# One read of the first batch's x, turned on TensorE; a weight conversion spread over three engines; a newly chosen instruction order

## The chip, the core and the metric

The kernel runs on one core of a Trainium2 chip. The core has five queues that run side by side, each strictly in its own order: TensorE (PE: matrix products and transposes, writing to PSUM), VectorE (DVE), ScalarE (ACT: functions of a table, and copies), GpSimd (POOL) and SyncE (SP), which here issues all DMA transfers. The metric is the device time of one execution in microseconds, median of several runs.

## What is computed

The reference is an attention through 32 inducing points over four batches of 12,480 tokens of 128 numbers, and behind it a two-layer network with a rational activation over all 49,920 tokens:

```python
def mab(q, kv):
    s = scale * (q @ kv.transpose(0, 2, 1))
    s = s - s.max(-1, keepdims=True)
    a = np.exp(s)
    a /= a.sum(-1, keepdims=True) + 1e-09
    return a @ kv
h = mab(I, x)                       # 32 points look at all tokens of a batch
x = mab(x, h)                       # every token looks at the 32 points
h = x @ w_in                        # 128 -> 2048
P = a[0] + a[1] * h + a[2] * h2 + a[3] * h3          # h2 = h*h, h3 = h2*h
Q = 1.0 + np.abs(b[0]) * np.abs(h) + np.abs(b[1]) * h2
out = (P / (Q + 1e-6)) @ w_out      # 2048 -> 128
```

`w_in` and `w_out` come as 64-bit floats and are turned into 32-bit ones on the chip, by work on their bits.

## The kernel before

A batch is cut into 26 tiles of 480 tokens (`BT`), four chunks of 120 each; seven groups of up to four tiles make the 32 points of a batch.

**The start** (`before`, lines 1235 to 1251, then `main` up to line 1292) is written out by hand and kept in program order (`pin`). For batch 0 x is read twice: by columns (`wide_columns`, `x_c`, 128 channels on the partitions) for the scores, and by rows (`wide_rows`, `x_t`, tokens on the partitions) for the weighted sum. For each group, `score` multiplies the points with the columns into the PSUM tile `pc`, takes the maximum on DVE (`mx`, `nm`), the exponential on ACT (`e`) and turns it with four PE transposes (`pt`, copied to `eT`); `weigh` multiplies `eT` with the rows (`ph`) and DVE adds to `acc`. `level`, the division and a last product give `HT0`, the points. Between these steps `step` deals out the conversion of the weights (`convert_weights`): four parts of `w_in` of 480 columns and one of 128, five parts of `w_out` of 384 and one of 128, seven DVE instructions each, the tiles named `cv` and `cw`. `warm` lets PE multiply the identity (`spare`) where it would wait. When the points are there, a flag decides on the branch; all that follows is the branch `main(True)`. It converts the last two parts of `w_out`, makes the first tokens' attention (`tokens`, `pd`, `a`, `pa`, `at`), the first pieces of the stacked first layer (`pg`, `gs`, `st`), scales `w_out` by a number (line 1287) and hands over to the flow.

**The block** (`Flow`) is all the rest: 832 units, each one tile of 480 tokens and two of the 16 row blocks of the hidden layer. PE makes `h` (two products, `first`); |h| goes to a buffer of `rooms` by ACT (`abs`) or, for the masked half of the units, by DVE (`mask`) or ACT (`taken`); DVE multiplies (`D`) into a slot `l`. A masked unit needs a constant added first: either POOL does it (`pre`, a tensor_scalar `l<-rooms,all`), or PE adds it to `h` with two more products with a constant matrix (`shift`, `h<-at,bump`). ACT takes a logarithm over one to four rooms at once (`ln`; a room holds two units, 1920 columns), and behind a change of function table a sigmoid: over a room (`sig2`), over one unit (`sig`), or into PSUM (`sigp`, tile `i`). Units whose sigmoid is in PSUM are ended by DVE (`Ev`), the others by two POOL instructions (`add`, `Eg`). PE multiplies with `w_out` (`second`, tile `po`, four records per unit). Attention for later tokens and batches is mixed in.

Which engine takes what, and in which order, is decided while the program is built, by `Flow.run`: it keeps a clock for each engine, moves it on by `COST`, and of what is ready picks by the weights `RANK`, `GEN`, `WAIT` and `LOAD`, of which a row of `SETS` is put in force for each 16 units (`PLAN`). The tables change only the order and the choice among `shift` and `pre`, `mask` and `taken`, `Ev` and `Eg`, `ln` over one room or several.

## Time and profile before

| | |
|---|---|
| median of 3 runs | 2232.44 us (2232.06 to 2234.06) |
| the profiled execution | 2232.32 us, span of its instructions 2230.4 us |
| busy: PE, DVE, ACT, POOL | 97%, 91%, 95%, 86% of the span |
| weight loads of PE (PEld) | 55% |
| chain that ended last | PE 48%, ACT 18%, POOL 15%, DVE 9%, issue 6%, DMA 2% |
| DMA | 82.59 MB read, 25.56 MB written |

Busy is the union of the instructions' durations, whatever they wait for inside. Neighbouring instructions of DVE and ACT overlap in the records by some 0.06 to 0.1 us; where the distance from start to start matters, it is read from a list in order of time. A PE record's end is modelled; the granted clock of PE is given as a share of 2.4 GHz, so 0.5 is 1.2 GHz.

### The profile page before, as it was taken

How to read it: one execution, taken by the hardware profiler on the slowest of the kernel's cores; microseconds unless marked ns; L12 is line 12 of the kernel's file. 1: busy time of each engine (PE TensorE's matmuls, PEld its weight loads, DVE VectorE, ACT ScalarE, POOL GpSimd, SP SyncE). 2: the span in 40 equal slices, each digit the busy share in tenths (PEclk: the TensorE clock that was granted, in tenths of full speed). 3: DMA queues.
4: the chain of work that ended last, by engine and by line, in shares of the span. 5: the costliest groups of instructions: out<-in, count | busy, mean ns of one | idle time of the engine just before them, and what ended most of it. 6: DMA issues, size and time to landing. Idle time of an engine off the chain costs nothing.

```text
span 2230.4 us, 24813 instructions
## 1 busy us (share of the span) xinstructions
PE 2158.1 (97%) x8210; PEld 1236.5 (55%) x8210; DVE 2028.7 (91%) x2208; ACT 2108.8 (95%) x1646; POOL 1917.0 (86%) x1279
## 2 busy tenths in 40 slices
PE   6899999999999999999999999999999999999998
PEld 3555555555655555655555555555555555555554
DVE  8798998999889999998999998989999999999996
ACT  2699999999999999999999999999999999999996
POOL 0479999997999898988899989999789989799884
PEclk9799999999999999999999999999999999999999
DMA  8122221211121212222112222221110111011000
GB/s 331 49 83 65 80 63 60 67 45 36 45 80 46 64 55 62 75 70 64 45 36 62 77 78 62 81 64 55 54 36 27 45 45 45 22 42 36 27 27 20
DMA packets 76937, 135.20 MB, mean 61 GB/s; under 512 B 13312, under 2 KB 63616, under 8 KB 76800
## 3 DMA queue, kind: packets, MB, share of 16 engines
q1 hardware_dynamic: 76800, 133.52, 19.2%
q8 instruction: 68, 1.11, 0.2%
q14 instruction: 69, 0.57, 0.1%
HBM read 82.59 MB, written 25.56 MB: 48 GB/s over the span
## 4 chain that ended last, share of the span: by engine, by line
PE 48%; ACT 18%; POOL 15%; DVE 9%; issue 6%; DMA 2%; SPq 0%; POOLq 0%; DVEq 0%; ACTq 0%
PE po L166 30%; POOL l L166 15%; ACT rooms L166 13%; PE h L166 11%; DVE l L166 6%; ACT i L166 3%; PE pd L166 2%; DVE rooms L166 2%; DMA rooms<-x_t 2%; PE ph L166 2%; ACT L166 1%; PE pc L166 1%; PE pl L166 1%; PE pgt L166 0%; DVE oT L166 0%
## 5 line engine op out<-in xcount | busy, mean ns | idle before, releaser
L166 PE MATMUL po<-l,w_out 128*128 128x480 f32 x3328 | 1466.4, 571 | 7.1 <-DVE oT L166 4.9
L166 POOL TENSOR_TENSOR l<-l,rooms 128x960 f32<-128x960 f32 x506 | 1136.0, 2245 | 71.5 <-ACT rooms L166 37.6
L166 PEld LDWEIGHTS po<-l,w_out 128*128 128x128 f32 x3328 | 616.3, 190 | 500.8 <-issue 435.9
L166 DVE SCALAR_TENSOR_TENSOR l<-rooms,all,h 128x960 f32<-128x960 f32 x648 | 770.7, 1206 | 55.2 <-ACT rooms L166 23.9
L166 ACT ACTIVATE rooms<-rooms,all 128x1920 f32<-128x1920 f32 (+3 forms) x286 | 743.4, 2621 | 3.9 <-POOL l L166 3.2
L166 PE MATMUL h<-at,st 128*128 128x480 f32 x1664 | 631.7, 475 | 29.6 <-DVE l L166 26.0
L166 POOL TENSOR_SCALAR l<-l,all 128x960 f32<-128x960 f32 x506 | 541.8, 1071 | 2.4
L166 DVE TENSOR_SCALAR rooms<-h 128x960 int32<-128x960 int32 x413 | 474.4, 1151 | 57.7 <-PE h L166 55.3
L166 ACT ACTIVATE rooms<-h,all 128x960 f32<-128x960 f32 x416 | 434.7, 1051 | 30.6 <-PE h L166 28.6
L166 ACT ACTIVATE rooms<-rooms 128x960 f32<-128x960 f32 (+1 forms) x331 | 461.0, 1417 | 0.2
L166 PEld LDWEIGHTS h<-at,st 128*128 128x128 f32 x1664 | 296.0, 190 | 288.9 <-issue 158.5
L166 DVE SCALAR_TENSOR_TENSOR l<-l,all,i 128x960 f32<-128x960 f32 x326 | 386.5, 1206 | 21.8 <-ACT i L166 20.7
L166 ACT ACTIVATE i<-rooms 128x960 f32<-128x960 f32 x326 | 310.3, 966 | 12.8 <-DVE l L166 11.2
L166 POOL TENSOR_SCALAR l<-rooms,all 128x960 f32<-128x960 f32 x184 | 196.6, 1069 | 136.9 <-DVE rooms L166 120.8
L166 DVE SCALAR_TENSOR_TENSOR l<-h,all,l 128x960 f32<-128x960 f32 x184 | 221.6, 1208 | 13.2 <-POOL l L166 11.4
L166 ACT ACT_TABLE_LOAD x140 | 179.6, 1283 | 3.2 <-PEq L1339 0.7
L166 PE MATMUL h<-at,bump 128*128 128x480 f32 x464 | 171.8, 452 | 3.8 <-DVE rooms L166 3.8
L166 PEld LDWEIGHTS h<-at,bump 128*128 128x128 f32 x464 | 84.0, 189 | 61.7 <-issue 26.2
L166 PEld LDWEIGHTS pd<-HT,xT 128*120 128x120 f32 x832 | 104.3, 187 | 18.2 <-issue 9.1
L166 PE MATMUL pd<-HT,xT 128*120 128x32 f32 x832 | 97.9, 262 | 1.9 <-ACT gs L166 1.4
L166 DVE COPY oT<-po 128x480 f32<-128x480 f32 x104 | 67.7, 651 | 24.8 <-PE po L166 24.2
L166 PE MATMUL po<-at,st 128*128 128x480 f32 x104 | 79.1, 760 | 0.0
(114 smaller groups left out, 700.2 us busy)
## 6 DMA issues: line engine op xcount, KB each, us to landing
xT<-x_c SPq DMA_DIRECT2D x182, 240.0 KB, 3.4
out<-oT SPq DMA_DIRECT2D x104, 240.0 KB, 2.2
at<-hl SPq DMA_DIRECT2D x412, 60.0 KB, 2.0
...
rooms<-x_c SPq DMA_DIRECT2D x5, 960.0 KB, 13.3
...
```

The costliest lines, as they stand in the source:

```text
L166: ins = call(*args, **kw)
```

## The change

Batch 0 is read by rows alone (`first_rows`, nine transfers into the rooms 9 to 1, the first in three pieces). `turned` makes the columns on the chip: for each tile four PE transposes into PSUM (`px`, two tiles to a PSUM buffer), and an ACT copy of 960 columns to `xc`. It runs two groups ahead of the scores. The parts of `w_out` land in rooms 0, 9 and 8. A conversion has now five DVE instructions, one on ACT (`cw<-raw`, the low word) and two on POOL (product and sum), and the last DVE instruction of a part comes one part later. The five parts of `w_in` are dealt out in the start, five steps a group; all six parts of `w_out` are converted behind the branch, the rest of them in one go (`step(60)`), and the scaling of `w_out` moves from DVE to POOL. `COST` of most instructions is raised (`first` 0.44 to 0.48, `shift` 0.44 to 0.47, `second` 1.61 to 1.63), all rows of `SETS` are new, and `PLAN` repeats another of them.

```diff
--- before.py
+++ after.py
@@ convert_weights
-    c = pool.tile([P, width], I32, tag=tags[1], name=f"cw{name}", bufs=1)
-    V = nc.vector
+    r = pool.tile([P, 2, width], I32, tag=tags[1], name=f"cw{name}", bufs=1)
+    c, l = r[:, 0], r[:, 1].bitcast(F32)
+    V, G = nc.vector, nc.gpsimd
     af, bf = a.bitcast(F32), b.bitcast(F32)
     yield V.tensor_scalar(out=a, in0=hi, scalar1=0x07FFFFFF, scalar2=3, op0=ALU.bitwise_and, op1=ALU.logical_shift_left)
+    nc.scalar.activation(l, lo.bitcast(U32), AF.Identity, bias=0.0, scale=2.0 ** -52)
     yield V.scalar_tensor_tensor(out=a, in0=hi, scalar=-0x40000000, in1=a, op0=ALU.bitwise_and, op1=ALU.bitwise_or)
     yield V.tensor_scalar(out=b, in0=a, scalar1=-0x00800000, scalar2=None, op0=ALU.bitwise_and)
-    yield V.scalar_tensor_tensor(out=bf, in0=lo.bitcast(U32), scalar=2.0 ** -52, in1=bf, op0=ALU.mult, op1=ALU.mult)
+    G.tensor_tensor(out=bf, in0=bf, in1=l, op=ALU.mult)
+    G.tensor_tensor(out=bf, in0=bf, in1=af, op=ALU.add)
     yield V.tensor_scalar(out=c, in0=hi, scalar1=0x7FF00000, scalar2=None, op0=ALU.bitwise_and)
-    yield V.tensor_tensor(out=bf, in0=bf, in1=af, op=ALU.add)
+    yield None
     yield V.scalar_tensor_tensor(out=dst, in0=c, scalar=float(0x38100000), in1=bf, op0=ALU.is_ge, op1=ALU.mult)
@@ class Flow
-    COST = {"first": 0.44, "second": 1.61, "linear": 0.22, "fetch": 0.57, "D": 1.125, "mask": 1.067, "Ev": 1.125, "abs": 0.944, "taken": 0.85, "ln": 1.79, "sig": 1.694, "half": 0.894, "load": 1.295, "both": 3.39, "pre": 1.04, "add": 1.12, "Eg": 2.215, "shift": 0.44}
+    COST = {"first": 0.48, "second": 1.63, "linear": 0.22, "fetch": 0.58, "D": 1.14, "mask": 1.085, "Ev": 1.135, "abs": 0.953, "taken": 0.85, "ln": 1.79, "sig": 1.694, "half": 0.894, "load": 1.295, "both": 3.39, "pre": 1.05, "add": 1.155, "Eg": 2.225, "shift": 0.47}
...
-        (77.9, 124, -279.1, 100.3, -37.2, -206.1, -83.4, 15.5, 61, 42.1, -224.4, 138.8, 408.6, 142.1, 24.5, 5.2, 59.4, 108.4, -17.2, -196.8, 18.8, 155, 103.5, -281.3, 0.07, 0.06, 0.06, 0.15, 0.25, -2.08, 210.6, 102.3),
+        (69.7, 124, -262.9, 108.4, -97.4, -198.7, -83.4, 13.3, 32.6, 47.2, -213.9, 108.5, 409, 149.2, 14.2, 4.9, 76.4, 108.4, -13.5, -190.6, 17.9, 162.6, 45.1, -281.3, 0.07, 0.06, 0.06, 0.09, -0.41, -1.54, 193.5, 106.1),
...
-        self.stretch, self.near = -1, -1
+        self.stretch, self.near = -1, 0
@@ class Kernel
-    STEPS = 8, 11, 11, 11, 11, 8, 3
+    STEPS = 5, 5, 5, 5, 5, 5, 0
-        nc.sync.dma_start(out=self.ind, in_=self.ind_c)
...
-            if n == len(parts) - 2:
-                yield None
-            raw = self.mp.tile([P, width], mybir.dt.int64, tag=self.place("l"), name=f"raw{n}", bufs=1)
+            if n < 5:
+                raw = self.mp.tile([P, width], mybir.dt.int64, tag=f"l{n}", name=f"raw{n}", bufs=1)
+            else:
+                t = self.rooms[:, (0, 0, 9, 9, 8, 8)[n - 5], n % 2].rearrange("p a n -> p (a n)")
+                raw = t[:, 0:2 * width].bitcast(mybir.dt.int64)
...
+    def first_rows(self):
+        for k in range(-(-self.NB // 3)):
+            n, m = 3 * k, min(3, self.NB - 3 * k)
+            t = self.rooms[:, Flow.ROOMS - 1 - k].rearrange("p a b n -> p (a b n)")[:, 0:m * HB * C].rearrange("p (m h c) -> p m h c", h=HB, c=C)
+            for lo, hi in ([(j, j + 1) for j in range(m)] if k == 0 else [(0, m)]):
+                self.nc.sync.dma_start(out=t[:, lo:hi].rearrange("p m h c -> p (m h) c"), in_=self.x_t[0, :, HB * (n + lo):HB * (n + hi), :])
+                if k == 0:
+                    yield
+            self.rows += [t[0:TP, j] for j in range(m)]
+            yield
+    def turned(self, g):
+        nc, xs, cols = self.nc, self.rows[4 * g:4 * g + 4], []
+        for h in range(0, len(xs), 2):
+            m = min(2, len(xs) - h)
+            px = self.ps_h.tile([P, 2, 512], F32, tag=f"hp{h // 2}", name=f"px{g}_{h}", bufs=1)
+            for j in range(m):
+                for c in range(HB):
+                    nc.tensor.transpose(out=px[:, j, TP * c:TP * c + TP], in_=xs[h + j][:, c, :], identity=self.ident[0:TP, 0:TP])
+            t = self.mp.tile([P, 2, BT], F32, tag=f"l{15 + (2 * g + h // 2) % 6}", name=f"xc{g}_{h}", bufs=1)
+            nc.scalar.activation(t[:, 0:m], px[:, 0:m, 0:BT], AF.Identity, bias=0.0, scale=1.0)
+            cols += [t[:, j] for j in range(m)]
+        return cols
+    def first_scores(self, g, cols, state):
+        nc, ap, nb = self.nc, self.ap, self.count(g)
+        X, scale, rows = mybir.AxisListType.X, 1.0 / math.sqrt(C), slice(0, M * nb)
+        pc = self.ps_m.tile([P, 512], F32, tag="misc", name=f"pc0_{g}")
+        for j, t in enumerate(cols):
+            nc.tensor.matmul(pc[M * j:M * j + M, 0:BT], self.ind, t, start=True, stop=True)
+        mx = ap.tile([P, 1], F32, tag="mx", name=f"mx0_{g}")
+        nc.vector.tensor_reduce(out=mx[rows], in_=pc[rows, 0:BT], axis=X, op=ALU.max)
+        old, nm = state["nm"], ap.tile([P, 1], F32, tag="nm", name=f"nm0_{g}", bufs=2)
+        state["nm"] = nm
+        if g == 0:
+            nc.vector.tensor_scalar(out=nm, in0=mx, scalar1=-scale, scalar2=None, op0=ALU.mult)
+        else:
+            if nb < 4:
+                nc.vector.tensor_copy(out=nm, in_=old)
+            nc.vector.tensor_scalar(out=nm[rows], in0=mx[rows], scalar1=-scale, scalar2=old[rows], op0=ALU.mult, op1=ALU.min)
+        e = ap.tile([P, BT], F32, tag="e", name=f"e0_{g}")
+        sums = ap.tile([P, 1], F32, tag="sums", name=f"sums0_{g}", bufs=3)
+        nc.scalar.activation(e[rows], pc[rows, 0:BT], AF.Exp, bias=nm[rows], scale=scale, accum_out=sums[rows])
+        cor = None
+        if g:
+            cor = ap.tile([P, 1], F32, tag="cor", name=f"cor0_{g}", bufs=2)
+            nc.scalar.activation(cor[rows], old[rows], AF.Exp, bias=nm[rows], scale=-1.0)
+        return e, sums, cor
+    def first_turn(self, g, e):
+        nc, rows = self.nc, slice(0, M * self.count(g))
+        pt = self.ps_h.tile([P, 2, 512], F32, tag="hp2", name=f"pt0_{g}", bufs=1)[:, 0].rearrange("p (c n) -> p c n", c=HB)
+        for c in range(HB):
+            nc.tensor.transpose(out=pt[0:TP, c, rows], in_=e[rows, TP * c:TP * c + TP], identity=self.ident[rows, rows])
+        eT = self.ap.tile([P, 512], F32, tag="gs", name=f"eT0_{g}", bufs=2)[0:TP].rearrange("p (c n) -> p c n", c=HB)
+        nc.scalar.activation(eT[:, :, rows], pt[0:TP, :, rows], AF.Identity, bias=0.0, scale=1.0)
+        return eT
+    def first_weigh(self, g, eT, sums, cor, acc):
+        nc, V, nb = self.nc, self.nc.vector, self.count(g)
+        rows, xs = slice(0, M * nb), self.rows[4 * g:4 * g + 4]
+        ph = self.ps_o.tile([P, 512], F32, tag="po", name=f"ph0_{g}")
+        for c in range(HB):
+            for j in range(nb):
+                nc.tensor.matmul(ph[M * j:M * j + M, 0:C], eT[:, c, M * j:M * j + M], xs[j][:, c, :], start=(c == 0), stop=(c == HB - 1))
+        if g == 0:
+            V.tensor_copy(out=acc[:, 0:C], in_=ph[:, 0:C])
+            V.tensor_copy(out=acc[:, C:], in_=sums)
+        else:
+            V.scalar_tensor_tensor(out=acc[rows, 0:C], in0=acc[rows, 0:C], scalar=cor[rows], in1=ph[rows, 0:C], op0=ALU.mult, op1=ALU.add)
+            V.scalar_tensor_tensor(out=acc[rows, C:], in0=acc[rows, C:], scalar=cor[rows], in1=sums[rows], op0=ALU.mult, op1=ALU.add)
+    def first_points(self):
+        self.rows, loads = [], self.first_rows()
+        for _ in range(3):
+            next(loads)
+        self.nc.sync.dma_start(out=self.ind, in_=self.ind_c)
+        self.fetch_words(1)
+        for _ in loads:
+            self.fetch_words(len(self.raw) < 5)
+        self.fetch_words(2)
+        acc = self.ap.tile([P, C + 1], F32, tag="acc", name="acc0")
+        state = {"acc": acc, "nm": None}
+        last, cols = self.NG - 1, {0: self.turned(0), 1: self.turned(1)}
+        old = None
+        self.conversion = self.converting([self.raw.pop(0) for _ in range(5)])
+        for g in range(self.NG):
+            e, sums, cor = self.first_scores(g, cols.pop(g), state)
+            self.step(self.STEPS[g])
+            if old is not None:
+                self.first_weigh(g - 1, *old, acc)
+            self.fetch_words(2 if 1 < g < 4 else 0)
+            if g + 2 <= last:
+                cols[g + 2] = self.turned(g + 2)
+            elif g == last:
+                self.open_spare("spare0")
+                self.warm(4)
+            old = self.first_turn(g, e), sums, cor
+        level = self.level(0, state["nm"])
+        self.until_bank(level, 2)
+        self.step(60)
+        self.first_weigh(last, *old, acc)
+        self.drive(self.points(0, state, level, self.cp.tile([C, 4 * M], F32, name="HT0")))
...
-    def converting(self):
-        while True:
-            if not self.raw:
-                return
-            tags = self.place("l"), self.place("l")
-            yield from convert_weights(self.nc, self.mp, *self.raw.pop(0), self.converted, tags)
-            self.converted += 1
+    def converting(self, parts):
+        last = None
+        while parts or last is not None:
+            this = None
+            if parts:
+                tags = [f"l{11 + 2 * (self.converted % 2) + i}" for i in range(2)]
+                this = convert_weights(self.nc, self.mp, *parts.pop(0), self.converted, tags)
+                self.converted += 1
+                for done in this:
+                    if done is None:
+                        break
+                    yield
+            if last is not None:
+                next(last)
+                yield
+            last = this
@@ before, main
-        self.drive(self.induce(0, self.cp.tile([C, 4 * M], F32, name="HT0")))
+        self.first_points()
-        self.fetch_words(2)
-        self.conversion = self.converting()
+        self.conversion = self.converting(list(self.raw))
-            self.step(20)
-            nc.vector.tensor_scalar(out=self.w_out, in0=self.w_out, scalar1=p.rho, scalar2=None, op0=ALU.mult)
+            self.step(60)
+            nc.gpsimd.tensor_scalar(out=self.w_out, in0=self.w_out, scalar1=p.rho, scalar2=0.0, op0=ALU.mult, op1=ALU.add)

```

Counted in the branch taken, the new order holds (records of PE and instructions of the others):

| | before | after |
|---|---|---|
| PE `h<-at,bump` (two to a `shift`) | 464 | 386 |
| POOL `pre` | 184 | 223 |
| POOL `add` and `Eg` pairs | 506 | 491 |
| DVE `Ev`, ACT `sigp` | 326 | 341 |
| DVE `mask` / ACT `taken` | 413 / 3 | 407 / 9 |
| ACT `ln` over 1, 2, 3, 4 rooms | 190, 69, 20, 7 | 254, 55, 12, 4 |
| ACT `sig2` / `sig` | 175 / 156 | 157 / 177 |
| ACT copies to `eT`, on 120x512 (the rest by DVE) | 27 | 35 |

How the start moves is shown at three places. On PE, around the third group's scores in the start, before (`pc` scores, `ph` weighted sums, `pt` turned exponentials; L166 and L169 are the line of the helper that records every instruction):

```order
L166 MATMUL pc_2_217<-rooms,ind 32x480 x4
L166 MATMUL ph_1_246<-rooms,eT_1_208 32x128 x16
L166 MATMUL pt_2_265<-ident,e_2_226 120x128 x4
L166 MATMUL pc_3_276<-rooms,ind 32x480 x4
L166 MATMUL ph_2_303<-rooms,eT_2_270 32x128 x16
```

The same place after (`px` are the transposes of x, `xc` the copies of them that the scores read):

```order
L169 MATMUL pc_2_295<-xc_0_203,ind 32x480 x2
L169 MATMUL pc_2_295<-xc_2_214,ind 32x480 x2
L169 MATMUL ph_1_319<-rooms,eT_1_293 32x128 x16
L169 MATMUL px_0_340<-ident,rooms 128x120 x8
L169 MATMUL px_2_351<-ident,rooms 128x120 x8
L169 MATMUL pt_2_362<-ident,e_2_304 120x128 x4
L169 MATMUL pc_3_369<-xc_0_275,ind 32x480 x2
L169 MATMUL pc_3_369<-xc_2_286,ind 32x480 x2
```

Sixteen transposes have come between the weighted sum of one group and the turned exponentials of the next. On DVE behind the branch, from the first token's attention to the first instruction of the block (`TENSOR_SCALAR rooms<-h` is the first `mask`), before:

```order
L166 TENSOR_TENSOR at_0_0_705<-pa_0_696,at_0_0_705 32x480 x2
L166 TENSOR_SCALAR cv_723<-raw_656 128x128
L166 SCALAR_TENSOR_TENSOR cv_723<-raw_656,cv_723 128x128
L166 TENSOR_SCALAR cv_723<-cv_723 128x128
L166 SCALAR_TENSOR_TENSOR cv_723<-raw_656,cv_723 128x128
L166 TENSOR_SCALAR cw_724<-raw_656 128x128
L166 TENSOR_TENSOR cv_723<-cv_723 128x128
L166 SCALAR_TENSOR_TENSOR w_out<-cw_724,cv_723 128x128
L166 TENSOR_SCALAR w_out<-w_out,all 128x2048
L166 TENSOR_SCALAR rooms<-h_0_2_742 128x960
```

The same place after: 23 conversion instructions stand between `at` and the first `mask`, of which these are the last eleven:

```order
L169 TENSOR_SCALAR cv_847<-rooms 128x384
L169 SCALAR_TENSOR_TENSOR cv_847<-rooms,cv_847 128x384
L169 TENSOR_SCALAR cv_847<-cv_847 128x384
L169 TENSOR_SCALAR cw_848<-rooms 128x384
L169 SCALAR_TENSOR_TENSOR w_out<-cw_838,cv_837 128x384
L169 TENSOR_SCALAR cv_857<-rooms 128x128
L169 SCALAR_TENSOR_TENSOR cv_857<-rooms,cv_857 128x128
L169 TENSOR_SCALAR cv_857<-cv_857 128x128
L169 TENSOR_SCALAR cw_858<-rooms 128x128
L169 SCALAR_TENSOR_TENSOR w_out<-cw_848,cv_847 128x384
L169 SCALAR_TENSOR_TENSOR w_out<-cw_858,cv_857 128x128
L169 TENSOR_SCALAR rooms<-h_0_2_878 128x960
```

The seven conversion instructions and the scaling between `at` and the first `mask` have become 23 conversion instructions. On POOL behind the branch, up to the first `pre` (`TENSOR_SCALAR l<-rooms,all`), before:

```order
L166 TENSOR_TENSOR bump<-level,bump 64x128
L166 TENSOR_TENSOR st_645<-gs_0_686,st_645 64x512
L166 TENSOR_TENSOR st_645<-gs_1_712,st_645 64x512
L166 TENSOR_SCALAR l_0_0_750<-rooms,all 128x960
L166 TENSOR_SCALAR l_0_2_755<-rooms,all 128x960
```

And after, the last twelve rows up to the first `pre`:

```order
L169 TENSOR_TENSOR cv_799<-cv_799,cw_800 128x384
L169 TENSOR_TENSOR cv_799<-cv_799 128x384
L169 TENSOR_TENSOR cv_827<-cv_827,cw_828 128x384
L169 TENSOR_TENSOR cv_827<-cv_827 128x384
L169 TENSOR_TENSOR cv_837<-cv_837,cw_838 128x384
L169 TENSOR_TENSOR cv_837<-cv_837 128x384
L169 TENSOR_TENSOR cv_847<-cv_847,cw_848 128x384
L169 TENSOR_TENSOR cv_847<-cv_847 128x384
L169 TENSOR_TENSOR cv_857<-cv_857,cw_858 128x128
L169 TENSOR_TENSOR cv_857<-cv_857 128x128
L169 TENSOR_SCALAR w_out<-w_out,all 128x2048
L169 TENSOR_SCALAR l_0_0_886<-rooms,all 128x960
```

Before the first `pre` POOL has now twelve conversion products and sums and the scaling of `w_out` over 2048 columns.

## Rows read from the trace of the kernel before

**Rows 1.** Chain that ended last, by engine, from the page.

```profile
PE 48%; ACT 18%; POOL 15%; DVE 9%; issue 6%; DMA 2%; SPq 0%; POOLq 0%; DVEq 0%; ACTq 0%
```

**Rows 2.** Windows: stretch, length, busy us of PE, PEld, DVE, ACT, POOL; clock, DMA, GB/s.

```profile
0.00:10.00 10.00, 3.07 (x8) 0.55 (x8) 4.28 (x63) 1.69 (x3) 0.68 (x6) 1.00 0.56 191
20.00:30.00 10.00, 8.15 (x74) 3.95 (x66) 9.61 (x21) 2.13 (x5) 0.00 (x0) 1.00 1.03 417
160.00:2200.00 2040.00, 2005.15 (x7413) 1144.63 (x7413) 1885.58 (x1891) 1998.65 (x1528) 1851.99 (x1226) 1.00 0.18 54
```

**Rows 3.** Chain that ended last, in order of time: start, length, what.

```profile
30.21 13.35 DMA rooms<-x_t
```

**Rows 4.** PE in order of time, start: start, length, instructions.

```profile
39.95 1.11 PE L166 MATMUL pt<-ident,e 128*120 128x128 f32 x4
...
44.60 0.66 PE L166 MATMUL pt<-ident,e 128*120 128x128 f32 x4
45.19 1.00 PE L166 MATMUL pc<-rooms,ind 128*32 128x480 f32 x4
46.12 1.60 PE L166 MATMUL spare<-ident 128*128 128x128 f32 x12
47.66 1.08 PE L166 MATMUL ph<-rooms,eT 120*32 120x128 f32 x32
```

**Rows 5.** DVE in order of time, from the end of the start on.

```profile
48.70 0.54 DVE L166 TENSOR_TENSOR cv<-cv 128x384 f32<-128x384 f32 x1
...
54.94 0.29 DVE L166 COPY HT<-HT 128x128 f32<-128x128 f32 x1 [0.64 <-PE HT L166]
...
56.13 0.56 DVE L166 SCALAR_TENSOR_TENSOR cv<-raw,cv 128x384 int32<-128x384 int32 x1
56.73 0.36 DVE L166 TENSOR_SCALAR cv<-cv 128x384 int32<-128x384 int32 x1
...
59.68 1.63 DVE L166 TENSOR_TENSOR cv<-cv 128x384 f32<-128x384 f32 x1
...
65.49 1.98 DVE L166 TENSOR_SCALAR w_out<-w_out,all 128x2048 f32<-128x2048 f32 x1
...
68.45 1.20 DVE L166 SCALAR_TENSOR_TENSOR l<-rooms,all,h 128x960 f32<-128x960 f32 x1
```

**Rows 6.** POOL in order of time, the same stretch.

```profile
59.52 1.37 POOL L166 TENSOR_TENSOR st<-gs,st 64x512 fp32r<-64x512 f32 x1 [5.33 <-ACT st L166]
...
65.27 1.12 POOL L166 TENSOR_SCALAR l<-rooms,all 128x960 f32<-128x960 f32 x1 [1.47 <-DVE cv L166]
```

**Rows 7.** POOL groups, 160 to 2200 us: count, busy us, mean ns, idle before.

```profile
L166 POOL TENSOR_TENSOR l<-l,rooms 128x960 f32<-128x960 f32 x494 | 1109.2, 2245 | 67.9 <-ACT rooms L166 34.9 <-POOL l L166 0.2
...
L166 POOL TENSOR_SCALAR l<-rooms,all 128x960 f32<-128x960 f32 x172 | 183.8, 1069 | 105.5 <-DVE rooms L166 92.8 <-PE po L166 6.5 <-ACT rooms L166 4.5
```

**Rows 8.** PE in order of time, in the block: one shift and what follows.

```profile
1016.47 0.60 PE L166 MATMUL h<-at,bump 128*128 128x480 f32 x2
1016.90 0.56 PE L166 MATMUL po<-l,w_out 128*128 128x480 f32 x1
```

**Rows 9.** ACT groups, 160 to 2200 us.

```profile
L166 ACT ACTIVATE rooms<-h,all 128x960 f32<-128x960 f32 x399 | 417.0, 1051 | 20.8 <-PE h L166 18.8 <-issue 0.3
L166 ACT ACTIVATE rooms<-rooms,all 128x1920 f32<-128x1920 f32 x179 | 335.7, 1893 | 3.8 <-POOL l L166 3.2 <-DVE l L166 0.4
L166 ACT ACTIVATE rooms<-rooms 128x1920 f32<-128x1920 f32 x170 | 302.8, 1795 | 0.2
L166 ACT ACTIVATE i<-rooms 128x960 f32<-128x960 f32 x309 | 294.2, 965 | 9.8 <-DVE l L166 8.5
L166 ACT ACTIVATE rooms<-rooms,all 128x3840 f32<-128x3840 f32 x68 | 237.5, 3494 | 0.0
...
L166 ACT ACTIVATE rooms<-rooms 128x960 f32<-128x960 f32 x153 | 151.8, 992 | 0.0
```

**Rows 10.** DVE group of `Ev`, 160 to 2200 us.

```profile
L166 DVE SCALAR_TENSOR_TENSOR l<-l,all,i 128x960 f32<-128x960 f32 x309 | 366.7, 1207 | 17.4 <-ACT i L166 16.2
```

More of the change, by code (lines that the diff above doesn't have):

```diff
@@ L741, in score @@
             nc.tensor.matmul(pc[M * j:M * j + M, 0:BT], self.ind, t, start=True, stop=True)
-        if not self.boot:
-            yield "unring", 0
+        yield "unring", 0
         yield "v", 0.57
@@ L757, in score @@
         e = ap.tile([P, BT], F32, tag="e", name=f"e{b}_{g}")
[L758 to L762 removed]
+        nc.scalar.activation(e[rows], pc[rows, 0:BT], AF.Exp, bias=nm[rows], scale=scale)
         yield "free", 0
@@ L868, in induce, with points @@
             yield from self.weigh(b, g, xs, state)
-        level = self.level(b, state["nm"])
-        if self.boot:
-            self.until_bank(level, 2)
-            self.step(20)
-            self.warm(1)
-            self.drive(self.weigh(b, self.NG - 1, rs[4 * self.NG - 4:], state))
+        yield from self.points(b, state, self.level(b, state["nm"]))
+    def points(self, b, state, level, own=None):
+        nc, ap, acc = self.nc, self.ap, state["acc"]
         cor = yield from level
@@ L999, in tokens @@
             for j in range(nb):
-                yield "pe", 0.75
+                yield "pe", 0.9
                 if j == 0:
```

59 lines of the change are left out of this document (5 added, 54 removed), and 98 rows, old and new, of the table SETS.

## The prediction

> **What bounds the kernel now.** I read the page first, then windows, the chain of waits, each engine's groups, and last the lists in order of time around the start. The page's chain goes to and fro: PE 48%, ACT 18%, POOL 15%, DVE 9% [rows 1], so no single engine sets the block. The windows say how little each could give back: of the 2040 us from 160 to 2200, PE is busy 2005, ACT 1999, DVE 1886, POOL 1852 [rows 2]. PE's figure is partly made by modelled ends; ACT's is real work, so ACT has 41 us of pause and is at least as tight as PE. The start is another case: from 10 us on the DMA share is full at 417 GB/s [rows 2], and the chain of waits is a transfer of x from 30.21 to 43.56 [rows 3]. The points are there with the copy of `HT` at 54.94, and the first product of the block on DVE begins at 68.45 [rows 5].
>
> Three terms follow: when the points are there, how long after them the block begins, and how long the block takes. The sum is made against the profiled execution, 2232.3 us, which is 0.1 below the median.
>
> **Term one, the points.** Reading x once takes 6.8 MB out of the queue: x by rows and `w_in` are 8.9 MB by their shapes. With 1.91 MB moved in the first 10 us and 0.417 MB/us from there [rows 2], all of x is in SBUF at 27 us instead of 43.6. But the scores of the first group stand on PE behind the transposes of the second, whose last tiles have 3.85 MB up to and with them in the queue: 14.7 us, and the first scores at about 15.9. From there PE has, for a group, the scores (0.93, from 45.19 to 46.12), the weighted sum (1.08), four transposes of exponentials (0.59, from 44.60 to 45.19) and sixteen new ones, by the same row 4 x 0.59 = 2.4: 4.9 us [rows 4]. ACT has two new copies of 960 columns, by the nearest group about 1.05 each [rows 9], which still leaves its group below PE's. Four groups at 4.9, one with half the transposes at 3.7, and one without at 3.3 (there the round from PE over DVE and ACT and back sets the time) bring the last scores to 42.5; before they began at 45.19. From there to `HT` it was 9.75 us, of which 1.5 were the warm-up products from 46.12 to 47.66 [rows 4, 5]; so `HT` would come at 50.7, 4.2 earlier. That holds at PE's full pace. The four transposes took 1.11 us at 39.95 and 0.66 at 44.60 [rows 4]: 1.7 times as long while PE still paused for x. At that pace throughout, the groups cost some 18 us more and `HT` is 14 late. PE would now pause little from 16 us on, as it did around 45; I let one group of the six run at the slow pace (3.4 us) and take **-1**, with ends at -5 and +8.
>
> **Term two, from the points to the block.** Here stands what the start has put off: all six parts of `w_out`, 30 DVE instructions instead of 14, and 12 POOL instructions instead of none. DVE alone: a part of 384 columns has three tensor_scalars at 0.36 and two of two inputs at 0.56 [rows 5]; less 0.08 of overlap each that is 1.8 us, 9.9 for the six parts with the narrow one. Before it was 2.8 and 1.4 for two parts, and 1.1 for the scaling without its wait: 5.3. So DVE's own work grows by 4.6. POOL: a product of two inputs over 960 columns takes 2.245 [rows 7], so I estimate 0.9 over 384, and 9.6 us for the twelve. The two cannot run beside each other freely. The DVE sum over 384 columns took 0.54 at 48.70, with POOL idle, and 1.63 at 59.68, while POOL's instruction of 59.52 ran for 1.37; the scaling took 1.98 at 65.49, beside POOL's of 65.27 [rows 5, 6]: DVE began when POOL was done, both times. These are a sum of two SBUF inputs and a one-input tensor_scalar; no row shows a scalar_tensor_tensor beside POOL. If all five of a part are held, DVE and POOL take turns: 9.9 and 9.6, and about 4 us of first-token work and 1 of waits, put the first `mask` at some 24 us behind `HT` and the first product at 25.5; before it was 13.5. That is +12. If only the three tensor_scalars are held, it is +9. If none is, POOL's own queue sets it, about 5 us until its first product, two splits of 1.37 and 9.6: the first product 19 us behind, +5.5. I take **+11**, the ends are +5 and +15. What hid the work before was the long transfer of x, beside which DVE converted; that cover is gone. Behind it POOL still scales `w_out` (1.069 x 2048/960 = 2.3 us [rows 7]) ahead of the first `pre`; DVE's first masks and the units without a mask need no `pre` and hide it, so I count nothing; without that cover it is 2.3.
>
> The Trainium skill, SBUF — State Buffer, section "Who interferes with whom", has a rule on this: a DVE instruction with two SBUF inputs, or in a mode that uses both ports, is locked out for the whole of a GpSimd instruction that reads SBUF, and the other way round. The two waits above agree; by the rule all five instructions of a part are held, and the term would be +12.
>
> **Term three, the block.** 39 shifts leave PE; two products and on to the next take 0.43 [rows 8], so PE loses 16.8 us. POOL gains 39 `pre` and loses 15 pairs: 39 x 1.07 - 15 x (2.245 + 1.07) = -8 [rows 7], the second figure of a pair by the form of `pre`. DVE gains 15 `Ev` at 1.2 [rows 10] and gives up six masks and eight copies, some +8. ACT grows: 39 logarithms more over the same 416 rooms, each split costing 2 x 1.893 - 3.494 = 0.29, are 11 at most and 8 with the overlap taken out; 15 sigmoids to PSUM and 21 single ones for 18 over a room are 15 x 0.965 + 21 x 0.992 - 18 x 1.795 = +3; six `taken` at 1.05 are 6; copies shifted between ACT and DVE about +1 [rows 9]. Together +18 on an engine with 41 us of pause. So PE's relief is a gain of up to 17 and ACT's load a loss of up to 18, on two engines that are alike in pause; I put the term at **0**, with both as ends.
>
> The sum: -1 + 11 + 0 = +10, **2242 us**. Its own range, with term two at its ends and term three within 4, is 2234 to 2252.
>
> **Rivals.**
> PE sets the block. For it: half the chain is PE, and its products with `w_out` come first in that chain [rows 1]. Against it: ACT would need to run with 23 us of pause where it has 41. Then 17 come back; with the points 4 early and the block beginning +6 to +8 behind them, the time is 2232 - 17 - 4 + 7 = 2218; with a part of the relief lost, 2221. This is the faster case, and it decides from 10 us of relief on.
>
> ACT sets the block. For it: 1999 of 2040 busy, and its largest pauses are 19 us for PE's `h` and 9 for DVE [rows 9], so little is left to squeeze. Then the term is +18 and the time 2260, or 2257 if the points come at -4.
>
> The Trainium skill's front page (Trainium Kernel Development and Optimization, "Performance Expectations") calls matmul busy time a bad measure and weight-load time a good one. By the weight loads, 1145 of 2040, PE is far from full, which speaks for this rival.
>
> The two cancel: the block gives back 10 and the start takes it, 2232. The change of the read then does what it says and is not seen.
>
> The start gains as it was cut to: no holding between DVE and POOL, PE at full pace, -5 and +5 in the first two terms. With term three at 0 that is 2232 too, and I count it with the case above.
>
> **How the numbers follow.** Forecast 0.41, PE sets the block 0.27, ACT sets it 0.17, cancelled 0.15. What a measurement of this kernel can tell from no change is about 0.2%, 4.5 us. The forecast's own range begins at +2, so a small part of it (0.03) is no change, and a part of the cancelled case (0.02) is faster. Faster 0.29, within 0.2% 0.16, slower 0.55. The range leaves out a tenth on each side: 2215, where PE's relief comes back whole and the points are early, to 2260, where ACT sets the block.
>
> **What would show it.** Term one: the `HT` copy on DVE, forecast at 54, and the distance of the scores `pc` from group to group, 4.9 us at full pace. Term two: the distance from there to the first product `l<-rooms,all,h`, 24 to 26 us, with conversions on DVE of 1 us and more where 0.36 and 0.56 are their own, lying against POOL's products. Term three: the time from the first `po` to the end, and ACT's pause between 160 and 2200, forecast at no more than 30 us. I am wrong if `HT` comes before 50, if the first product comes less than 19 us behind it, or if the block alone is more than 8 us shorter or longer.

## The result, and the profile after

The changed kernel takes 2259.36 us (median of 4 runs, 2257.45 to 2260.51) against 2232.57: the ratio is 1.0118, with a 95% interval from 1.0101 to 1.0136. It is slower, as forecast, but by 26.8 us where +10 was forecast. The profiled execution took 2257.45 us with a span of 2255.6, 25.2 more than before; it is the fastest of the four, so the spans below account for 25 of the 26.8 us.

Two points cut that span into the prediction's three terms: the copy of `HT` on DVE, and the first product on DVE behind it.

| | before | after | term | forecast |
|---|---|---|---|---|
| `HT` copied | 54.94 | 55.03 | +0.1 | -1 (-5 to +8) |
| from there to the first product | 13.51 | 26.16 | +12.65 | +11 (+5 to +15) |
| from there to the end of the span | 2161.95 | 2174.41 | +12.5 | 0 (-17 to +18) |

The windows of the kernel after (stretch, length, busy us of PE, PEld, DVE, ACT, POOL; clock, DMA, GB/s), which answer to [rows 2]; the row of 81.19 begins at the first product and is the block:

```profile
20.00:30.00 10.00, 8.95 (x122) 6.50 (x121) 9.32 (x19) 7.67 (x14) 5.22 (x4) 1.00 1.02 409
70.00:80.00 10.00, 0.06 (x1) 0.06 (x1) 8.85 (x16) 3.76 (x7) 6.14 (x7) 0.50 0.00 0
81.19:2255.60 2174.41, 2116.03 (x7750) 1200.37 (x7750) 1976.57 (x1986) 2102.85 (x1668) 1905.03 (x1280) 0.99 0.18 54
160.00:2200.00 2040.00, 1997.88 (x7342) 1130.31 (x7341) 1881.46 (x1887) 2006.43 (x1588) 1830.76 (x1229) 1.00 0.18 54
```

And the same stretch, from the first product on, of the kernel before:

```profile
68.45:2230.40 2161.95, 2112.33 (x7825) 1210.27 (x7825) 1972.06 (x1982) 2088.53 (x1600) 1912.08 (x1269) 0.99 0.18 54
```

In the block PE has 75 records less and is busy 3.7 us *longer*; its pauses have grown from 49.6 to 58.4. ACT is busy 14.3 longer and pauses 1.9 less: seen from ACT, the block has grown by ACT's own work. That this work is the cause is not shown by these two rows; it is tested below. From 160 to 2200, ACT pauses 33.6 us (41 before). The chain of the page, by engine, answers to [rows 1]; ACT's share was 18%:

```profile
PE 40%; ACT 30%; DVE 13%; issue 9%; POOL 8%; DMA 1%; SPq 0%; DVEq 0%; ACTq 0%; POOLq 0%
```

The groups of ACT from 160 to 2200 (count, busy us, mean ns, idle before) show where its work comes from, against [rows 9]: logarithms over one room, and sigmoids of one unit:

```profile
L169 ACT ACTIVATE rooms<-rooms,all 128x1920 f32<-128x1920 f32 x242 | 454.0, 1894 | 3.5 <-DVE l L169 3.0 <-DVE nm L169 0.3
...
L169 ACT ACTIVATE i<-rooms 128x960 f32<-128x960 f32 x319 | 302.7, 964 | 10.7 <-DVE l L169 9.6
L169 ACT ACTIVATE rooms<-rooms 128x1920 f32<-128x1920 f32 x151 | 269.3, 1796 | 0.2
L169 ACT ACTIVATE rooms<-rooms,all 128x3840 f32<-128x3840 f32 x55 | 192.2, 3497 | 0.1
L169 ACT ACTIVATE rooms<-rooms 128x960 f32<-128x960 f32 x171 | 169.7, 993 | 0.0
```

One group of the start on PE (start, length, instructions), which answers to [rows 4], and the last scores:

```profile
25.29 1.86 PE L169 MATMUL px<-ident,rooms 120*128 120x120 f32 x16
26.98 0.60 PE L169 MATMUL pt<-ident,e 128*120 128x128 f32 x4
27.52 1.01 PE L169 MATMUL pc<-xc,ind 128*32 128x480 f32 x8
28.74 1.08 PE L169 MATMUL ph<-rooms,eT 120*32 120x128 f32 x32 [0.21 <-ACT eT L169]
29.75 1.86 PE L169 MATMUL px<-ident,rooms 120*128 120x120 f32 x16
...
45.32 1.00 PE L169 MATMUL pc<-xc,ind 128*32 128x480 f32 x4
```

The scores stand 4.5 to 5.1 us apart, as forecast (4.9), at the full clock. But the first came at 17.87 instead of 15.9, and the last are 9.7 from `HT`, as before; the 1.5 that I took off for the warm-up products did not come, since PE waits there for the exponentials and not for itself. So the early read was lost in full against this profile of before. That profile is the earliest of its kind, though: in the nine runs below whose start is word for word that of before, `HT` is copied between 55.06 and 57.84, and with the one before the ten have a mean of 55.9. The changed start puts it between 54.82 and 55.07 in four runs. In the old start the granted clock lies at 0.5 for 7 to 24 us of the first 50, while PE pauses for x; in the changed one it is 1.00 up to 60.

Behind the points, on DVE: `HT`, one part of `w_out`, and the first product, against [rows 5]:

```profile
55.03 0.29 DVE L169 COPY HT<-HT 128x128 f32<-128x128 f32 x1 [0.64 <-PE HT L169]
...
69.72 1.04 DVE L169 TENSOR_SCALAR cv<-rooms 128x384 int32<-128x384 int32 x1
70.80 0.56 DVE L169 SCALAR_TENSOR_TENSOR cv<-rooms,cv 128x384 int32<-128x384 int32 x1
71.39 0.36 DVE L169 TENSOR_SCALAR cv<-cv 128x384 int32<-128x384 int32 x1
71.67 0.35 DVE L169 TENSOR_SCALAR cw<-rooms 128x384 int32<-128x384 int32 x1
71.94 1.37 DVE L169 SCALAR_TENSOR_TENSOR w_out<-cw,cv 128x384 f32<-128x384 int32 x1
...
81.19 1.21 DVE L169 SCALAR_TENSOR_TENSOR l<-rooms,all,h 128x960 f32<-128x960 f32 x1
```

And POOL in the same place, against [rows 6]:

```profile
69.36 1.19 POOL L169 TENSOR_TENSOR cv<-cv 128x384 f32<-128x384 f32 x1
71.89 0.99 POOL L169 TENSOR_TENSOR cv<-cv,cw 128x384 f32<-128x384 f32 x1 [1.35 <-DVE cv L169]
```

The first tensor_scalar of a part takes 1.04 where its like takes 0.36: it ends 0.2 behind POOL's sum of 69.36. The last instruction takes 1.37 instead of 0.56, beside POOL's product of 71.89. A part costs 3.61 us on DVE, and six of them, one narrow, stand there. (In the second part, from 59 us on, other instructions are held as well.) PE meanwhile has nothing: from 67.2 to 79.9 it waits for `gs`, whose copies stand on ACT behind the conversions of `cw`; its granted clock is 0.50 all through that pause and until 106 us (before, from 69 to 93).

### The profile page after: what moved, and what is told of

Its sections match the earlier page's. It is cut to its first block, busy times and chain, and to the rows that moved or that the text cites. A ratio compares the mean times of both kernels' runs of the same rounds, so it can differ in the third digit from the quotient of the medians.

```text
span 2255.6 us, 25006 instructions
## 1 busy us (share of the span) xinstructions
PE 2165.4 (96%) x8226; PEld 1235.3 (55%) x8226; DVE 2033.6 (90%) x2189; ACT 2139.3 (95%) x1738; POOL 1932.9 (86%) x1311
## 4 chain that ended last, share of the span: by engine, by line
PE 40%; ACT 30%; DVE 13%; issue 9%; POOL 8%; DMA 1%; SPq 0%; DVEq 0%; ACTq 0%; POOLq 0%
PE po L169 25%; ACT rooms L169 22%; PE h L169 9%; DVE l L169 7%; POOL l L169 7%; ACT i L169 4%; ACT L169 2%; DVE rooms L169 2%; PE ph L169 2%; PE pd L169 1%; PE pc L169 1%; DVE cv L169 1%; PE pgt L169 0%; DMA at<-hl 0%; SPq L169 0%
## 5 line engine op out<-in xcount | busy, mean ns | idle before, releaser
L169 PE MATMUL po<-l,w_out 128*128 128x480 f32 x3328 | 1465.2, 572 | 6.8 <-POOL l L169 3.3
L169 POOL TENSOR_TENSOR l<-l,rooms 128x960 f32<-128x960 f32 x491 | 1102.0, 2244 | 66.8 <-ACT rooms L169 35.4
L169 PEld LDWEIGHTS po<-l,w_out 128*128 128x128 f32 x3328 | 618.6, 190 | 512.0 <-issue 448.4
L169 DVE SCALAR_TENSOR_TENSOR l<-rooms,all,h 128x960 f32<-128x960 f32 x609 | 725.9, 1205 | 54.2 <-ACT rooms L169 42.5
L169 ACT ACTIVATE rooms<-rooms,all 128x1920 f32<-128x1920 f32 (+3 forms) x325 | 755.4, 2343 | 3.7 <-DVE l L169 3.0
L169 PE MATMUL h<-at,st 128*128 128x480 f32 x1664 | 620.9, 470 | 39.0 <-DVE l L169 30.4
L169 POOL TENSOR_SCALAR l<-l,all 128x960 f32<-128x960 f32 x491 | 525.7, 1071 | 2.4
L169 DVE TENSOR_SCALAR rooms<-h 128x960 int32<-128x960 int32 x407 | 465.7, 1150 | 49.6 <-PE h L169 48.3
L169 ACT ACTIVATE rooms<-h,all 128x960 f32<-128x960 f32 x416 | 434.9, 1051 | 27.3 <-PE h L169 25.9
L169 PEld LDWEIGHTS h<-at,st 128*128 128x128 f32 x1664 | 294.5, 191 | 300.8 <-issue 154.7
L169 ACT ACTIVATE rooms<-rooms 128x960 f32<-128x960 f32 (+1 forms) x334 | 450.7, 1370 | 0.2
L169 DVE SCALAR_TENSOR_TENSOR l<-l,all,i 128x960 f32<-128x960 f32 x341 | 403.5, 1207 | 24.9 <-ACT i L169 24.0
L169 POOL TENSOR_SCALAR l<-rooms,all 128x960 f32<-128x960 f32 x223 | 238.1, 1068 | 140.5 <-DVE rooms L169 122.9
L169 ACT ACTIVATE i<-rooms 128x960 f32<-128x960 f32 x341 | 323.5, 964 | 13.4 <-DVE l L169 12.0
L169 DVE SCALAR_TENSOR_TENSOR l<-h,all,l 128x960 f32<-128x960 f32 x223 | 268.3, 1207 | 10.8 <-POOL l L169 8.6
L169 PE MATMUL h<-at,bump 128*128 128x480 f32 x386 | 145.0, 459 | 2.6 <-DVE rooms L169 2.3
L169 PEld LDWEIGHTS pd<-HT,xT 128*120 128x120 f32 x832 | 107.9, 192 | 28.1 <-ACT gs L169 14.3
L169 PE MATMUL pd<-HT,xT 128*120 128x32 f32 x832 | 100.9, 267 | 12.7 <-ACT gs L169 12.7
L169 PEld LDWEIGHTS h<-at,bump 128*128 128x128 f32 x386 | 68.2, 190 | 59.5 <-DVE rooms L169 33.5
L169 DVE COPY oT<-po 128x480 f32<-128x480 f32 x104 | 67.6, 650 | 19.4 <-PE po L169 19.0
L169 PE MATMUL po<-at,st 128*128 128x480 f32 x104 | 78.8, 758 | 0.0
```

The lines of the kernel that those rows point to most:

```text
L169: ins = call(*args, **kw)
```

## The experiments

All times are medians; the kernel before, run beside them on the same chip, lay between 2232.5 and 2233.3. "Block" is the time from the first product on DVE to the end of the span (before: 2162.0).

**The two halves apart.** The start alone: the changed kernel with the planner's tables and attention cost of before, so that the block has the old order.

```diff
-    COST = {"first": 0.48, ...
+    COST = {"first": 0.44, ...
...
-                yield "pe", 0.9
+                yield "pe", 0.75
```

> The new start with the planner's old tables, so that the block has word for word the order of the kernel before. Theory (start and block lose apart from each other): the points at 55, the first product of the block on DVE at 81 and from there the block's old length (2162 us from the first product to the end), 2245 us, 2243 to 2247. Rival 1 (the new order was fitted to the late start, the old order suffers behind it): 2250 us or more. Rival 2 (the block makes good a part of a late start): 2238 us or less.

Measured: 2244.87 us, ratio 1.0050 (1.0036 to 1.0064). The points at 54.91, the first product at 81.09, the block 2164.3. And the order alone, the same edit the other way round in the kernel before:

> The old start with the planner's new costs and tables, so that the block has word for word the order of the changed kernel. Theory (the new order carries more ScalarE work and ScalarE sets the block): the first product at 68.5 as before, the block longer by 12.5 us, 2245 us, 2242 to 2248. Rival 1 (the new order is only bad behind the late start): 2230 to 2236 us. Rival 2 (TensorE sets the block, the new order's loss comes from the rest of the start): below 2232 us.

Measured: 2243.41 us, ratio 1.0042 (1.0028 to 1.0055), the block 2171.3 long:

```profile
70.02:2241.30 2171.28, 2116.78 (x7747) 1201.16 (x7747) 1976.99 (x1986) 2102.74 (x1668) 1902.91 (x1278) 0.99 0.18 54
```

Each half loses by itself, 11.6 and 10.1 us; the theory held for both in size. In the order alone, the 545th unit's product with `w_out` still begins 3.9 us earlier than before (1521.0 against 1524.9); the loss arises behind it. There, up to 1779, ACT waits 5.2 us for DVE's products ahead of the sigmoids into PSUM, where it waited 0.5 over the same units before. The block behind that product, before, in the changed kernel, and in the changed kernel with less work on ACT (`act_less_after` below):

```profile
1524.90:2230.40 705.50, 685.46 (x2289) 386.02 (x2289) 644.00 (x632) 679.36 (x516) 606.74 (x401) 1.00 0.12 36
1532.40:2255.60 723.20, 691.58 (x2314) 383.25 (x2313) 654.31 (x645) 689.22 (x555) 614.42 (x413) 0.99 0.13 40
1527.20:2247.60 720.40, 691.55 (x2314) 384.43 (x2313) 654.50 (x645) 685.48 (x555) 615.01 (x413) 0.99 0.13 40
```

The changed kernel is 5.2 us ahead of before at that product and loses 17.7 behind it; ACT is busy 9.9 us longer there, and it also pauses 7.8 us longer. One place in the order alone shows what such pauses can come from. A DVE instruction of the stacked first layer is held beside a POOL product, 2.36 us where it takes 0.43 at 1660.48; DVE's next products come late, ACT waits 1.46 us and PE 0.77 and 1.38 for them, and then the granted clock is at 0.5 for 10 us, in which eight products with `w_out` take 5.89 us where four take 1.77 at the full clock:

```profile
1638.75 2.36 DVE L166 TENSOR_SCALAR st<-gs 128x512 fp32r<-128x512 f32 x1
...
1638.57 2.26 POOL L166 TENSOR_TENSOR l<-l,rooms 128x960 f32<-128x960 f32 x1
...
1645.19 1.14 PE L166 MATMUL h<-at,st 128*128 128x480 f32 x2 [1.38 <-DVE l L166]
...
1645.00:1655.00 10.00, 9.81 (x27) 6.78 (x28) 8.22 (x10) 7.95 (x9) 8.24 (x6) 0.51 0.05 18
```

Between 160 and 2200 us the clock is at 0.5 for 10 to 20 us in each of the five runs of the new order, not at all in the kernel before or in `ln_split_all` below, and for at most 7 us in any other run. That may be why PE is busy longer with fewer products. What the hold and the clock cost the block was not measured by itself. A delay of the start is carried through the block whole: nothing in it makes it good. The sum of the halves is 21.7, so about 5 us belong to their meeting (the block of the changed kernel is 3 us longer than in the order alone, nearly all of it behind the 545th unit's product); where these come from was not tried.

**Does ScalarE's work set the block?** First more of it in the old order: 39 merged logarithms split, and then all of them.

```diff
-            A.activation(t, t, AF.Ln, bias=p.lam, scale=LAM)
+            if m > 1 and k.cut < 39:        # the second kernel: < 999
+                k.cut += m - 1
+                for j in range(i, i + m):
+                    t = k.rooms[:, j].rearrange("p a b n -> p (a b n)")
+                    A.activation(t, t, AF.Ln, bias=p.lam, scale=LAM)
+            else:
+                A.activation(t, t, AF.Ln, bias=p.lam, scale=LAM)
```

> The kernel before with 39 logarithm instructions more over the same rooms (the first merged ones are split into one per room), order otherwise unmoved. If ScalarE sets the block, the split costs 39 x 0.2 to 0.29 = 8 to 11 us: 2240 to 2244 us. If TensorE sets it, ScalarE's pauses take it up: 2232 to 2235 us.

Measured: 2236.09 us, ratio 1.0011 (1.0002 to 1.0020): between the two. ACT's busy time grew by 6.8 us only (0.17 for a split, not 0.29), and the block by 3.0. All of them split:

> The kernel before with every merged logarithm split into one per room: 130 instructions more, at the 0.17 us of busy time that the first 39 cost, 22 us of ScalarE, order otherwise unmoved. If ScalarE's work is a load that the old order can take up by half only: 2242 to 2248 us. If its pauses (73 us in the block) take it up: 2233 to 2236 us. If ScalarE sets the block from some point on, so that the loss grows faster than the load: 2250 us or more.

Measured: 2242.88 us, ratio 1.0047 (1.0033 to 1.0061):

```profile
71.38:2244.30 2172.92, 2115.64 (x7825) 1207.13 (x7825) 1973.55 (x1982) 2109.94 (x1730) 1912.36 (x1269) 0.99 0.18 54
```

ACT is busy 21.4 us longer, the block is 11.0 longer, with DVE and POOL within 1.5 us and PE 3.3 longer. So ACT's work alone makes a loss, at about half its length; for the 14.3 us of the change that would be 7, not the 12.5 seen.

Then less of it, in the new order and in the old:

```diff
+            t = k.rooms[:, i:i + m].rearrange("p r a b n -> p (r a b n)")[:, 0:1880 * m]
             A.activation(t, t, AF.Ln, bias=p.lam, scale=LAM)
```

> The changed kernel with each logarithm over 1880 instead of 1920 columns of a room (40 columns of each room stay without it), order unmoved: 416 x 40 x 0.83 ns = 13.9 us less of ScalarE, about what the change added to it in the block (14.3). Theory (ScalarE's added work is what the block lost): 2246 to 2250 us. Rival (the new order itself, its waits between the engines): 2255 us or more.

Measured: 2250.23 us, ratio to the kernel before 1.0082 (1.0068 to 1.0095), so 9 us back; ACT is busy 11.9 less in the block, and the block is 7.8 shorter:

```profile
81.00:2247.60 2166.60, 2113.61 (x7750) 1201.37 (x7750) 1976.55 (x1986) 2090.98 (x1668) 1907.89 (x1280) 0.99 0.18 54
```

That leaves 4.6 us of the block's 12.5, with 2.4 us of the added ACT work still there. The hold at `st<-gs` (2.37 us at 1644.94) and the lower clock (14 us) are in this run too.

> The same in the kernel before, 13.9 us less of ScalarE, order unmoved. If ScalarE sets the block there too: 2219 to 2224 us. If the old order had ScalarE and the others in balance, with pauses that take up half of a change as the split logarithms showed (6.8 us of ScalarE cost 3): 2225 to 2229 us. If ScalarE doesn't count there: 2231 us or more.

Measured: 2235.0 us, ratio 1.0007 (0.9998 to 1.0016): nothing. Its block begins 1.5 us later than before, has won back 1.0 of that by 1588 us, and there loses 3 at two small instructions on DVE:

```profile
1588.45 2.26 DVE L166 COPY low<-mt 1x128 f32<-1x128 f32 x1
...
1595.41 2.04 DVE L166 TENSOR_SCALAR acc<-acc,cor 128x129 f32<-128x129 f32 x1
```

beside POOL's

```profile
1588.40 2.24 POOL L166 TENSOR_TENSOR l<-l,rooms 128x960 f32<-128x960 f32 x1
...
1595.13 2.23 POOL L166 TENSOR_TENSOR l<-l,rooms 128x960 f32<-128x960 f32 x1
```

Both end when POOL's product does. Before, they fell differently against it, the copy 0.04 us ahead of POOL's product instead of 0.05 behind it, and took 0.21 and 0.89:

```profile
1587.95 0.21 DVE L166 COPY low<-mt 1x128 f32<-1x128 f32 x1
...
1592.87 0.89 DVE L166 TENSOR_SCALAR acc<-acc,cor 128x129 f32<-128x129 f32 x1
...
1587.99 2.29 POOL L166 TENSOR_TENSOR l<-l,rooms 128x960 f32<-128x960 f32 x1
```

**Does TensorE's relief count?** Every sixth shift is left out, in the old order and in the new.

```diff
     def shift(self, u):
+        self.left_out += 1
+        if self.left_out % 6 == 0:
+            return
```

> The kernel before with every sixth shift left out on TensorE (38 of 232 pairs of products, 0.43 us each, 16 us of TensorE; these units lack their added constant), order otherwise unmoved. If TensorE sets the block: 2216 us, and at most 2222. If ScalarE sets it: 2229 to 2232 us.

Measured: 2231.46 us, ratio 0.9990 (0.9981 to 0.9999); the block is 2.0 shorter for 16 us (10 by PE's busy time):

```profile
70.08:2230.00 2159.92, 2102.37 (x7749) 1195.09 (x7749) 1971.95 (x1982) 2088.81 (x1600) 1914.56 (x1269) 0.99 0.18 54
```

> The changed kernel with every sixth shift left out on TensorE (32 pairs, 13.8 us; these units lack their added constant), order unmoved. If ScalarE sets the block: 2256 to 2259 us. If TensorE does: 2246 to 2250 us.

Measured: 2254.81 us, ratio to before 1.0094 (1.0078 to 1.0109), 4.5 below the changed kernel with runs that lie up to 6 apart; in the profile, of one of the slower runs, the block is 1.1 shorter. TensorE sets the block in neither: 13.8 us of it bring back a third at most.

**What holds the old block, then?** Both reliefs together, each of the two other engines, and all four.

```diff
-            G.tensor_tensor(out=u.g, in0=u.g, in1=u.u, op=ALU.mult)
+            g, w = (t.rearrange("p a n -> p (a n)")[:, 0:948] for t in (u.g, u.u))
+            G.tensor_tensor(out=g, in0=g, in1=w, op=ALU.mult)
...
-            V.scalar_tensor_tensor(out=u.g, in0=u.g, scalar=p.k3, in1=u.inv, op0=ALU.add, op1=ALU.mult)
+            g, w = u.g[:, :, 0:462], u.inv[:, :, 0:462]
+            V.scalar_tensor_tensor(out=g, in0=g, scalar=p.k3, in1=w, op0=ALU.add, op1=ALU.mult)
```

> The kernel before with both reliefs at once: each logarithm over 1880 of 1920 columns (13.9 us of ScalarE) and every sixth shift left out on TensorE (16 us; those units lack their added constant), order unmoved. Alone the first gave nothing and the second 2 us. Theory (TensorE and ScalarE are in balance, so that one engine's relief only shows the other): together clearly more than the sum of both, 2220 to 2227 us. Rival (neither: fixed distances between dependent instructions of the old order set the block): 2229 us or more.

> The kernel before with GpSimd's last product of a unit over 948 instead of 960 columns (12 columns of it keep the unfinished value): 506 x 12 x 2.34 ns = 14 us less of GpSimd, order unmoved. If GpSimd's long pairs hold the block: 2222 to 2228 us. If not: 2230 us or more.

> The kernel before with VectorE's last product of a unit over 924 instead of 960 columns (36 columns keep the unfinished value): 326 x 36 x 1.04 ns = 12 us less of VectorE, order unmoved. If VectorE holds the block: 2222 to 2228 us. If not: 2230 us or more.

> The kernel before with all four reliefs at once (16 us of TensorE, 13.9 of ScalarE, 12 of VectorE, 14 of GpSimd; the columns and the added constants named in the single runs are left out), order unmoved. If the four engines are in balance and hand the block to each other: 2217 to 2224 us, clearly below each single run. If fixed distances or waits that no engine's work sets hold the block: 2228 us or more.

| relieved | us | ratio (interval) |
|---|---|---|
| PE and ACT | 2230.51 | 0.9990 (0.9981 to 0.9999) |
| POOL | 2235.07 | 1.0013 (1.0003 to 1.0022) |
| DVE | 2231.01 | 0.9994 (0.9985 to 1.0003) |
| all four | 2226.92 | 0.9975 (0.9966 to 0.9984) |

```profile
68.80:2225.10 2156.30, 2100.87 (x7749) 1197.79 (x7749) 1962.59 (x1982) 2075.15 (x1600) 1898.85 (x1269) 0.99 0.18 54
```

By these times my theory of a balance between PE and ACT fell with the first, POOL's relief made the kernel slower, and all four at once give 5.7 us for 12 to 16 us on each engine. But the profiles of `both_less` and `all_less` hold the same chance loss of some 3 us as `act_less_before`; here in `all_less`:

```profile
1581.66 2.17 DVE L166 COPY low<-mt 1x128 f32<-1x128 f32 x1
...
1588.53 1.97 DVE L166 TENSOR_SCALAR acc<-acc,cor 128x129 f32<-128x129 f32 x1 [0.21 <-ACT cor L166]
```

Ahead of it, from the block's first product to the 541st unit's product with `w_out` (1510 us before), the single reliefs have gained 1.6 (PE), 1.1 (ACT), 2.1 (POOL) and 1.4 us (DVE), PE and ACT together 3.5, and all four 6.4 (one profile each): every gain is small, and they roughly add up. So no engine sets the old order's block; the engines share it, PE and ACT are no special pair, and the times of these two runs are some 3 us too long to be read as what the reliefs are worth. Even with 3 us more all four give under 9 us; what holds the rest was not settled.

**The conversions behind the points.** The product and the sum back on DVE, nothing else moved:

```diff
-    V, G = nc.vector, nc.gpsimd
+    V, G = nc.vector, nc.vector
```

> The changed kernel with the product and the sum of each conversion on VectorE instead of GpSimd, nothing else moved. If the two engines hold each other, VectorE's 10 to 12 more instructions cost less than the waits: a full part takes 2.8 us instead of 3.6, the first product of the block comes at 76 to 78 instead of 81, 2254 to 2256 us. If they do not (VectorE is late by its own instructions), the first product comes at 83 or later, 2261 us or more.

Measured: 2256.87 us, ratio 1.0109 (1.0094 to 1.0125). Neither: `HT` came 1.3 later (56.33) and the first product at 80.89, 24.6 behind it instead of 26.2. One part on DVE:

```profile
70.81 0.36 DVE L169 TENSOR_SCALAR cv<-rooms 128x384 int32<-128x384 int32 x1
71.21 0.56 DVE L169 SCALAR_TENSOR_TENSOR cv<-rooms,cv 128x384 int32<-128x384 int32 x1
71.80 0.36 DVE L169 TENSOR_SCALAR cv<-cv 128x384 int32<-128x384 int32 x1
72.27 0.56 DVE L169 TENSOR_TENSOR cv<-cv,cw 128x384 f32<-128x384 f32 x1
72.86 0.56 DVE L169 TENSOR_TENSOR cv<-cv 128x384 f32<-128x384 f32 x1
73.34 0.35 DVE L169 TENSOR_SCALAR cw<-rooms 128x384 int32<-128x384 int32 x1
73.61 0.55 DVE L169 SCALAR_TENSOR_TENSOR w_out<-cw,cv 128x384 f32<-128x384 int32 x1
...
80.89 1.20 DVE L169 SCALAR_TENSOR_TENSOR l<-rooms,all,h 128x960 f32<-128x960 f32 x1
```

The instructions that were held take 0.36 and 0.55 again, so the hold is real; but two instructions more take back nearly all of it, 3.4 us a part against 3.6. Sharing a part with POOL bought nothing.

Last, the new read with the old order and the conversions put back into the start: seven DVE instructions again, two parts ahead of the first scores, where DVE idled, then one in each group.

```diff
-    STEPS = 5, 5, 5, 5, 5, 5, 0
+    STEPS, SOON = (7, 7, 7, 7, 7, 7, 3), 9
...
-        last, cols = self.NG - 1, {0: self.turned(0), 1: self.turned(1)}
+        last, cols = self.NG - 1, {0: self.turned(0)}
+        self.step(14)
+        cols[1] = self.turned(1)
```

> The new read of x with the old order of the block; the conversion is again seven VectorE instructions, two parts of w_in stand ahead of the first scores, one part in each group after them, so that nine of eleven parts are done in the start and two behind the points, as in the kernel before. Theory (the start lost because four parts more were put behind the points, not by the single read): the points at 54 to 57, the first product 12 to 14 behind them, 2228 to 2234 us. Rival (VectorE can't take them beside the groups: the points come late by what the parts take): the points at 60 or later, 2238 us or more.

Measured: 2232.65 us, ratio 1.0001 (0.9992 to 1.0010), with

```profile
57.05 0.29 DVE L166 COPY HT<-HT 128x128 f32<-128x128 f32 x1 [0.64 <-PE HT L166]
...
70.64 1.20 DVE L166 SCALAR_TENSOR_TENSOR l<-rooms,all,h 128x960 f32<-128x960 f32 x1
```

13.6 us lie between the two, and all that the start had lost is back: it was the four parts behind the points, not the single read. (This version also takes the conversion off POOL and ACT; off POOL alone, in the run above, it was worth 1.6 us of the 12.65.) A last try to win something over before moved the narrow part of `w_in` to the sixth group and left three parts behind the points:

> As the version with nine parts in the start, but with the narrow part of w_in moved to the sixth group and the fourth part of w_out put behind the points: eight parts in the start, three behind the points. If VectorE's conversions held the last groups up: the points at 54.5 to 55.5 instead of 57, the first product 14 to 15 behind them, 2230 to 2232 us. If not, the third part costs its 2.8 us: 2234 us or more.

Measured: 2234.44 us, ratio 1.0008 (0.9999 to 1.0017). The points came at 54.40, as meant, and the first product at 69.12, 14.7 behind them. The first product is 1.5 earlier than in the version above, but the profiled executions take the same time (2234.6 and 2234.8): the points answer to the first case, the time to the second. Of the kernels tried, none that does all the work beat the kernel before.

## Why the prediction was wrong

*Term one* (-1, measured +0.1; -0.9 between the means of ten old and four new starts): right within its range, for partly wrong reasons, and in part by luck. The pace of a group was right; what I had allowed for PE's slow clock was not needed (the granted clock is 1.00 up to 60 us), and that allowance of 3.4 hid that I had the first scores 2 us too early and the tail 1.5 too short.

*Term two* (+11, measured +12.65): right. DVE and POOL hold each other, as the two waits of [rows 5, 6] said. Once the parts follow each other, not all five instructions of a part are held but two, the first tensor_scalar and the last scalar_tensor_tensor; the others fall into POOL's pauses, and POOL into theirs. The rule of the Trainium skill (SBUF — State Buffer, "Who interferes with whom") agrees in kind with 1.04 beside 0.36 and 1.37 beside 0.56, though the prediction took it to hold all five; the +12 worked out that way is near the measured term.

*Term three* is the step that failed: "I put the term at **0**, with both as ends", PE's relief of up to 17 against ACT's load of up to 18. I took two engines for alike in pause, and so a relief on one and a load on the other for equal and opposite. The runs give each its own price. In the old order 16 us of PE are worth 2, and 12 us of ACT relief at most 1 before the hold took it back; ACT's load costs half its length (6.8 for 3.0, 21.4 for 11.0), and in the new order ACT's relief returns two thirds (11.9 for 7.8). ACT's load was 14.3 by busy time, where I had 18 (a split is 0.17, where the sum had 0.21; the rest of the difference was not traced). At those prices, which are carried over from other kernels, it makes 7 to 9 of the 12.5, and PE's relief would give back 2. The rest, 5 to 7 us, is not explained. The loss as a whole lies behind the 545th unit's product, where ACT's pauses grow by 7.8 us and the ACT relief returned only 2.8; the hold and the lower clock shown there are candidates, and no run took them away.

The rival "ACT sets the block" named the right engine and the right sign, but its condition is wrong too: ACT's load is not added whole. That its 2260 is the measured time is luck: 18 us of load at full price stand there for 14.3 at a lower price and the unexplained rest.

The range was also added up wrong: terms two and three at their ends give 2232 to 2250, not 2234 to 2252; the measured time lies above both. What the prediction named and did not put into its sum: PE's weight loads fill 55% of it, and its matmul time is modelled. And the chain's PE share does not say that PE would run ahead if it were freed.
